# Attention on one core: steps by kind of product, minima and exponentials ahead of the transposes

## The chip, the cores and the metric

One NeuronCore of a Trainium2 chip. Its engines work from queues of their own: TensorE (PE in the profile; PEld are its weight loads), VectorE (DVE), ScalarE (ACT), GpSimd (POOL) and SyncE (SP, which issues most DMAs). The metric is the device time of one execution in microseconds, the median of three runs.

## What is computed

Three stages in a row, in float32: attention with a decay that is summed along the sequence, a routed expert layer (each token goes to one of eight experts), and a dense layer with a squared ReLU.

```python
# attention: B, H, S, D = 4, 8, 576, 64
scores = q @ k.T / sqrt(D)
cum = cumsum(log(clip(f, 1e-4, 1)))
scores = where(causal, -1e9, scores + cum[:, None] - cum[None, :])
attn = exp(scores - max(scores)); attn /= sum(attn) + 1e-9
x = (attn @ v), heads side by side            # 2304 tokens x 512
# expert layer: 8 experts, 512 -> 1024 -> 512
e = argmax(x @ w_gate); gate = softmax(x @ w_gate)[e]
y = gate * sigmoid(x @ w_output_gate)[e] * (relu(x @ w1[e]) @ w2[e])
# dense layer: 512 -> 2048 -> 512
h = relu(y @ w_in); out = (h * h) @ w_out
```

## The kernel before

The order of all instructions is written out by hand: a generator of Python code emits them, and each engine keeps the order of emission. The change lies in the first stage, attention, with the routing of its tokens.

*Pairs, chunks and units.* Two heads form a pair; there are 16 pairs, four to a batch element (`NPAIR`, `HP`). The 576 query rows of a pair are cut into five chunks (`CH`): 64 rows and four of 128, and chunk i needs 64, 192, 320, 448 or 576 key columns. A unit is one chunk of one head, and `units` lists them in the order pair, chunk, head; the last three pairs (`KL`) put their chunks 0 to 2 first and mix two units of chunks 3 and 4 in between (`KM`).

*What a unit goes through.* `products` (L301) multiplies q by k for both heads of a chunk, head 0 from partitions 0 to 63 and head 1 from 64 to 127, each into a PSUM bank of the four in `R_S`, and adds the causal mask by small bf16 products (L314, L317). `scores` (L319) is a DVE instruction that adds the decay, writes the negated scores to `pbuf` and yields their minimum; 576 columns are two pieces of 288 (`columns`), the second of which takes the first one's minimum in. `expo` (L337) is ACT's exponential in place, with the row sum. `transp` (L346) turns the exponentials by PE into one of two banks (`R_T`), up to four blocks of 128 columns at a time, and `bal.copy` takes them to `pts` by DVE or ACT, whichever a running count of costs has less on. `pv` (L365) multiplies them by v: chunks 0 to 2 together form group 0 (320 columns at most), chunks 3 and 4 group 1 (256), into the one bank of `R_O`, with head 0 on the columns 0 to 63 of the array and head 1 on 64 to 127.

*The order.* `unit(n)` emits, for each n: the loads that fall due (L624 to L631: `loadcv` and `load` two pairs ahead, and the zero fill of the expert buffers `xs_d`), the scores of unit n, the transposes of unit n - 6 (`LAG`), the exponential of unit n, and one piece of `pv`, which starts two units behind its last transposes (`PVD`). After each unit one or two pieces (`FNR`) of the routing follow:

```python
            if LAG <= n < N + LAG:
                p, i, h = units[n - LAG]
                transp(p, i, h)
```

*Routing.* When the last pair of a batch element has its PV of a group, `finish(b, g)` (L394) starts: logits by PE (lp, 32 columns of the array), transposes of the attention output (xp) with a scaling on DVE (xr), transposes of the logits (lt), a maximum and its index by small DVE operations (lg, mx, te, me, oh), ranks by small products (rp), a position for each token, and a scatter by POOL. It is cut into pieces by `yield`. `lead` finds the expert with most tokens once three batch elements are routed, and `ranks` the order of all when the last one is.

*The tail.* Six more units empty the pipeline (L935 to L943), mixed with pieces of `fnq` (the routing) and of `bp`, which splits the first expert's weights into two parts (`prep`, L735: a cast on ACT and a subtraction on DVE). Then come the end of the routing, the first expert's early products and a loop for overflowing tokens, and the expert stage.

Of the kernel before, what the change touches and what calls it, by code (L numbers as in the profile page):

```python
# [8 lines left out]
F32 = mybir.dt.float32  # L9
# [11 lines left out]
P = 128  # L21
# [13 lines left out]
LAG, PVD, FNR = 6, 2, (1, 2)  # L35
# [17 lines left out]
KL, KM = 3, 2  # L53
# [88 lines left out]
def body(ctx, tc, cst, cst16, qkv, f_in, wl_in, w12, w34, out, dbg=None):  # L142
# [39 lines left out]
    R_S, R_T, R_O, R_F, R_H, R_X = (0, 1, 2, 3), (4, 5), (6,), (7,), (0, 1), (6, 7)  # L182
# [7 lines left out]
    ptp1 = alate.enter_context(tc.tile_pool(name="ptp1", bufs=2))  # L190
    vp = alate.enter_context(tc.tile_pool(name="vp", bufs=4))
    ptp0 = aearly.enter_context(tc.tile_pool(name="ptp0", bufs=2))
# [3 lines left out]
    if True:  # L196
# [39 lines left out]
        for k in range(2):  # L236
            for h in range(2):
                for i in range(NCH):
                    if k and i < 3:
                        pbuf[k, h, i] = pbuf[0, h, i]  # L240
                        continue
                    pb = pbuf[k, h, i] = (ap2 if i < 3 else ap1).tile([P, CH[i][2] + 64], F32, name=f"p{k}{h}{i}")
                    nc.gpsimd.memset(pb[:, CH[i][2]:], 0.0)
# [13 lines left out]
        def begin0():  # L257

            cumr = ap2.tile([B * H + 1, S], F32, name="cumr")
            def spread(h, a, z):  # L260

                pp = bank(R_S, "sp")
# [22 lines left out]
        units = [(p, i, h) for p in range(NPAIR - KL) for i in range(NCH) for h in range(2)]  # L285

        u1 = [(p, i, h) for p in range(NPAIR - KL, NPAIR) for i in (3, 4) for h in range(2)]
        for p in range(NPAIR - KL, NPAIR):
            units += [(p, i, h) for i in range(3) for h in range(2)]
            if p + 1 < NPAIR:  # L290
                units += [u1.pop(0) for _ in range(KM)]
        units += u1
        begin = {units.index((p, 0, 0)): p for p in range(NPAIR)}
        mns = {}
        pps = {}

        def columns(i):
            L = CH[i][2]
            return [(0, 288), (288, 576)] if L > 512 else [(0, L)]

        def products(p, i):  # L301
# [4 lines left out]
            for a, z in columns(i):  # L306
                pp = [bank(R_S, "sp") for _ in hs]
                pps[p, i, a] = pp
                for h, s in enumerate(hs):
                    nc.tensor.matmul(pp[h][:r, 0:z - a], lhsT=t[s, 0, q0:q0 + r], rhs=t[s, 1, a:z], start=True, stop=z < L)  # L310
# [8 lines left out]
        def scores(p, i, h):  # L319
# [4 lines left out]
            pb = pbuf[p % 2, h, i]  # L324
            mn = 3.0e38
            if h == 0:
                products(p, i)
            for a, z in columns(i):
# [8 lines left out]
        def expo(p, i, h):  # L337
            b, hp = divmod(p, HP)
            q0, r, L = CH[i]
            pb = pbuf[p % 2, h, i]  # L340
# [5 lines left out]
        def transp(p, i, h):  # L346
# [9 lines left out]
            for j0, j1 in ([(0, nb)] if nb <= 4 else [(0, 3), (3, 5)]):  # L356
                tp = bank(R_T if cur[0] < N else R_T + R_S, "tp", Q4)
# [868 lines left out]
```

## Time and profile before

| | us |
|---|---|
| runs | 908.23, 909.35, 910.71; median 909.35 |
| profiled execution | 907.29 |
| its span, first to last instruction | 905.2 |
| PE busy | 874.8 (97%) |
| DVE busy | 500.0 (55%) |
| ACT busy | 405.4 (45%) |
| POOL busy | 49.5 (5%) |

A row of the timeline is a merged run of instructions of one kind: its start, how long it lasts, the engine and line, the output and its inputs, the array's rows and columns, the shape of one and how many. The end of a run of matmuls includes the time until the last result is written, so the start of the next run, not the end, says when PE went on. A float32 product appears as two matmuls, so two heads of one chunk make four. A few matmul records are missing from the trace. In a row of waits stand the engine and what it waited for, the sum, how often and the longest.

### The profile page before, as it was taken

How to read it: one execution, taken by the hardware profiler on the slowest of the kernel's cores; microseconds unless marked ns; L12 is line 12 of the kernel's file. 1: busy time of each engine (PE TensorE's matmuls, PEld its weight loads, DVE VectorE, ACT ScalarE, POOL GpSimd, SP SyncE). 2: the span in 40 equal slices, each digit the busy share in tenths (PEclk: the TensorE clock that was granted, in tenths of full speed). 3: DMA queues.
4: the chain of work that ended last, by engine and by line, in shares of the span. 5: the costliest groups of instructions: out<-in, count | busy, mean ns of one | idle time of the engine just before them, and what ended most of it. 6: DMA issues, size and time to landing. Idle time of an engine off the chain costs nothing.

```text
span 905.2 us, 15024 instructions
## 1 busy us (share of the span) xinstructions
PE 874.8 (97%) x5642; PEld 751.8 (83%) x5642; DVE 500.0 (55%) x1271; ACT 405.4 (45%) x974; POOL 49.5 (5%) x125
## 2 busy tenths in 40 slices
PE   9999999999878999999999999999999999999997
PEld 5666666666678999999999799988989999999996
DVE  5677677776637778665667888423223233233222
ACT  7656656665315555545554455223223223223221
POOL 1001111020200000000000000001100100001001
PEclk9999999999889999999999999999999999999999
DMA  8874434313346767766555443002001001000000
GB/s 256 260 251 164 147 110 159 109 58 137 112 150 219 257 206 251 244 201 213 185 193 155 123 133 94 1 3 102 36 1 36 35 1 40 31 1 12 24 1 35
DMA packets 43060, 107.40 MB, mean 119 GB/s; under 512 B 8631, under 2 KB 16695, under 8 KB 42984
## 3 DMA queue, kind: packets, MB, share of 16 engines
q1 hardware_dynamic: 39784, 96.50, 32.9%
q0 software_dynamic: 2912, 9.60, 2.9%
q8 instruction: 46, 0.75, 0.4%
q10 hardware_dynamic: 288, 0.30, 0.1%
q14 instruction: 30, 0.25, 0.1%
HBM read 84.56 MB, written 21.82 MB: 118 GB/s over the span
## 4 chain that ended last, share of the span: by engine, by line
PE 44%; issue 21%; DVE 2%; DMA 2%; POOL 1%; ACT 1%; SPq 0%; POOLq 0%; DVEq 0%; ACTq 0%
PE ph L747 22%; PE py L791 12%; PE po L1118 10%; POOL out L1129 1%; DMA raw<-w 1%; PE xp L769 1%; DMA cm_d<-xw 1%; DVE rl L1110 0%; DVE lw L879 0%; ACT hs L1111 0%; DVE xT L1052 0%; DVE hs L1112 0%; SPq L833 0%; ACT rl L1108 0%; DVE mk L880 0%
## 5 line engine op out<-in xcount | busy, mean ns | idle before, releaser
L747 PE MATMUL ph<-xT,g 128*128 128x384 f32 (+9 forms) x1968 | 346.8, 325 | 5.5 <-DMA cm_d<-xw 5.1
L747 PEld LDWEIGHTS ph<-xT,g 128*128 128x128 f32 x1968 | 322.4, 190 | 14.8 <-issue 5.3
L1118 PE MATMUL po<-g,hs 128*128 128x512 f32 x864 | 216.0, 394 | 0.8 <-ACT hs L1111 0.7
L1118 PEld LDWEIGHTS po<-g,hs 128*128 128x128 f32 x864 | 160.6, 188 | 32.0 <-ACT hs L1111 1.4
L1110 DVE TENSOR_TENSOR rl<-ph,rl 128x384 f32<-128x384 f32 x96 | 53.3, 555 | 182.8 <-ACT rl L1108 182.8
L1108 ACT ACTIVATE rl<-ph 128x384 f32<-128x384 f32 x96 | 47.2, 492 | 196.0 <-PE ph L747 193.9
L791 PE MATMUL py<-hs,g 128*128 128x288 f32 (+8 forms) x816 | 126.6, 304 | 3.9 <-DVE hs L778 2.5
L791 PEld LDWEIGHTS py<-hs,g 128*128 128x128 f32 x816 | 118.2, 190 | 4.7 <-DVE hs L778 3.1
L342 ACT ACTIVATE p<-p,mn 64x64 f32<-64x64 f32 (+4 forms) x160 | 89.3, 559 | 24.4 <-DVE mn L331 24.1
L738 DVE TENSOR_TENSOR g<-raw,g 128x512 fp32r<-128x512 f32 x126 | 81.6, 687 | 15.1 <-ACT g L737 14.0
L1112 DVE TENSOR_TENSOR hs<-rl,hs 128x384 fp32r<-128x384 f32 x96 | 53.6, 558 | 55.7 <-ACT hs L1111 55.7
L1111 ACT CAST hs<-rl 128x384 fp32r<-128x384 f32 x96 | 49.3, 513 | 72.4 <-DVE rl L1110 72.3
L331 DVE CUSTOM_DVE_ANT_0 p<-sp,cb 64x64 f32<-64x64 f32 (+4 forms) x160 | 66.2, 422 | 24.8 <-PE sp L317 19.8
L359 PE MATMUL tp<-c,p 128*128 128x128 f32 (+1 forms) x480 | 74.5, 280 | 0.5 <-DVE g L129 0.4
L737 ACT CAST g<-raw 128x512 fp32r<-128x512 f32 x126 | 71.9, 619 | 6.2 <-DMA raw<-w 6.0
L310 PE MATMUL sp<-qk 64*128 64x288 f32 (+4 forms) x384 | 70.6, 426 | 2.8 <-DVE mn L331 2.8
L777 ACT ACTIVATE hs<-ph 128x288 fp32r<-128x288 f32 (+8 forms) x68 | 28.6, 421 | 94.7 <-PE ph L747 93.2
L129 ACT COPY g<-tp 128x256 f32<-128x256 f32 (+3 forms) x111 | 45.0, 408 | 54.3 <-PE tp L359 54.2
L376 PE MATMUL po<-g,v 128*64 128x256 f32 (+3 forms) x512 | 62.2, 366 | 1.2 <-DVE g L129 1.2
L778 DVE SCALAR_TENSOR_TENSOR hs<-ph,hs 128x288 fp32r<-128x288 f32 (+8 forms) x68 | 31.8, 467 | 57.0 <-ACT hs L777 56.9
L359 PEld LDWEIGHTS tp<-c,p 128*128 128x128 f32 (+1 forms) x480 | 50.9, 140 | 10.8 <-issue 3.1
L310 PEld LDWEIGHTS sp<-qk 64*128 64x128 f32 (+1 forms) x384 | 32.9, 176 | 27.1 <-issue 19.1
(136 smaller groups left out, 597.8 us busy)
## 6 DMA issues: line engine op xcount, KB each, us to landing
raw<-w SPq DMA_DIRECT2D x63, 512.0 KB
rawc<-w SPq DMA_DIRECT2D x32, 512.0 KB
qk<-qkv SPq DMA_DIRECT2D x15, 576.0 KB
cb<-cum_d SPq DMA_DIRECT2D x15, 576.0 KB
xs_d<-zt SPq DMA_DIRECT2D x8, 826.6 KB
v<-qkv SPq DMA_DIRECT2D x16, 320.0 KB
xT<-yT_d SPq DMA_DIRECT2D x6, 768.0 KB
xw<-xs_d SPq DMA_DIRECT2D x7, 529.0 KB
```

The source lines that it names most:

```text
L310: nc.tensor.matmul(pp[h][:r, 0:z - a], lhsT=t[s, 0, q0:q0 + r], rhs=t[s, 1, a:z], start=True, stop=z < L)
L331: nc.vector.tensor_tensor_reduce(out=pb[:r, a:z], in0=pp[:r, 0:z - a], in1=cb[:r, h, a:z], scale=-SCALE, scalar=mn, op0=ALU.add, op1=ALU.m ...
L342: nc.scalar.activation(out=pb[:r, 0:L], in_=pb[:r, 0:L], func=AF.Exp, bias=mns.pop((p, i, h)), scale=-1.0, accum_out=rss[b][:r, i, hh:hh + 1])
L359: nc.tensor.transpose(tp[:, j - j0, :r], pbuf[p % 2, h, i][:r, P * j:P * j + P], ident[:r, :r])
L376: nc.tensor.matmul(po[64 * h:64 * h + 64, a:W], lhsT=v[:, j, 64 * h:64 * h + 64], rhs=pts[p, h, g][:, j, a:W], start=(j == 0), stop=(j == ...
L737: nc.scalar.copy(g[:, 0, o:o + 512], raw)
L738: nc.vector.tensor_tensor(out=g[:, 1, o:o + 512], in0=raw, in1=g[:, 0, o:o + 512].bitcast(F32), op=ALU.subtract)
L747: nc.tensor.matmul(ph[:, :n], lhsT=g[:, a, kk * 256 + f * P:kk * 256 + f * P + P], rhs=x[:, c, kk, c0:c0 + n], start=(k == 0), stop=(k == 11))
L791: nc.tensor.matmul(py[c][:, c0:c0 + cap], lhsT=g[:, a, o:o + P], rhs=hs[:, x, :cap], start=(first and n == 0), stop=(last and n == 2 and e ...
L1110: nc.vector.tensor_tensor(out=rl, in0=ph[:, :CK], in1=rl, op=ALU.mult)
L1112: nc.vector.tensor_tensor(out=hs[:, 1, :CK], in0=rl, in1=hs[:, 0, :CK].bitcast(F32), op=ALU.subtract)
L1118: nc.tensor.matmul(po[t], lhsT=hs[:, x, t * P:(t + 1) * P], rhs=g[:, a, 1024 + f * 512:1536 + f * 512], start=(first and n == 0), stop=(la ...
```

## The change

A step now is a group of chunks of a pair, both heads: group 0 has six units, group 1 four (`GR`). Of the last three pairs the three group-0 steps come first, then the three of group 1. `step(n)` emits all score products of step n, the exponentials of the last two units of step n - 1 (`rest`), then minima and exponentials of step n except the last two exponentials, then the whole of PV of step n - 2, and last the transposes of step n - 1. Score products have fixed places: banks 0 and 1 hold chunks 0 and 1, or chunk 3 and the first 64 columns of chunk 4; banks 2 and 3 hold chunk 2, or the other 512 columns of chunk 4 (`COLS`). The transposes go through banks 4, 2, 5, 3, 4, 5 in turn. Chunk 0 is transposed with all 128 rows, of which the lower ones are zeros. Pieces of the routing that contain a product (`yield 1` ahead of them) stand behind the first or the last transposed unit of a step; others also ahead of PV, behind it and behind any transposed unit that takes no product. `pbuf` exists twice for all chunks, `pts` once.

```diff
-LAG, PVD, FNR = 6, 2, (1, 2)
+GR = ((0, 1, 2), (3, 4))
+FNR = (1, 2)
...
-    R_S, R_T, R_O, R_F, R_H, R_X = (0, 1, 2, 3), (4, 5), (6,), (7,), (0, 1), (6, 7)
+    R_S, R_T, R_O, R_F, R_H, R_X = (0, 1, 2, 3), (4, 2, 5, 3, 4, 5), (6,), (7,), (0, 1), (6, 7)
...
+        steps = [(p, g) for p in range(NPAIR - KL) for g in range(2)]
+        steps += [(p, g) for g in range(2) for p in range(NPAIR - KL, NPAIR)]
+        N = len(steps)
...
+        COLS = ([(0, 64, 0, 0)], [(0, 192, 0, 64)], [(0, 320, 1, 0)], [(0, 448, 0, 0)], [(0, 64, 0, 448), (64, 576, 1, 0)])
...
-                tp = bank(R_T if cur[0] < N else R_T + R_S, "tp", Q4)
+                tp = bank((R_T[turn_t[0] % len(R_T)],), "tp", Q4)
+                turn_t[0] += 1
                 for j in range(j0, j1):
-                    nc.tensor.transpose(tp[:, j - j0, :r], pbuf[p % 2, h, i][:r, P * j:P * j + P], ident[:r, :r])
+                    nc.tensor.transpose(tp[:, j - j0, :], pbuf[side[p, i], h, i][:, P * j:P * j + P], ident)
...
+        def follow(product):
+            while fnq and (product or not due.get(id(fnq[0]), 1)):
+                try:
+                    due[id(fnq[0])] = next(fnq[0])
+                    return
+                except StopIteration:
+                    fnq.pop(0)
...
+        def step(n, then=None):
+            cur[0] = n
+            new = units(n) if n < N else []
+            old = units(n - 1) if 1 <= n <= N else []
+            if new:
+                p, g = steps[n]
...
+                for i in GR[g]:
+                    side[p, i] = n % 2
+                    advance(first)
+                    products(p, i)
+                for k in range(6 * g, 6 * g + len(new)):
+                    loads(p, k)
+            while rest:
+                expo(*rest.pop(0))
+            for k, u in enumerate(new):
+                scores(*u)
+                if k < len(new) - 2:
+                    expo(*u)
+                else:
+                    rest.append(u)
+            follow(False)
+            if n >= 2:
+                pv(*steps[n - 2])
+            follow(False)
+            turn_t[0] = 0
+            for k, u in enumerate(old):
+                transp(*u)
+                if then:
+                    then()
+                else:
+                    follow(k in (0, len(old) - 1))
...
+    def between():
+        advance(fnq, TF)
+        for _ in range(2):
+            if tail[0] in PN:
+                next(bp)
+            tail[0] += 1
+
+    step(N, between)
+    step(N + 1, between)
```

On PE, in a pair without routing, before: the transposes of chunk 4 (tp, five blocks for each head) with the second part of a PV of group 0 (po) between them, and the scores (sp) of the next chunk.

```order
L359 MATMUL tp<-c_64,p_125 128x128 x5
L376 MATMUL po<-g_2119,v 64x192
L376 MATMUL po<-g_2128,v 64x192
L376 MATMUL po<-g_2119,v 64x128
L376 MATMUL po<-g_2128,v 64x128
L359 MATMUL tp<-c_64,p_135 128x128 x5
L310 MATMUL sp<-qk 128x448 x2
```

The same place after, from a whole PV of group 0 to the next step's scores.

```order
L379 MATMUL po<-g_2098,v 64x320
L379 MATMUL po<-g_2111,v 64x320
L379 MATMUL po<-g_2098,v 64x192
L379 MATMUL po<-g_2111,v 64x192
L379 MATMUL po<-g_2098,v 64x128
L379 MATMUL po<-g_2111,v 64x128
L361 MATMUL tp<-c_64,p_143 128x128 x4
L361 MATMUL tp<-c_64,p_153 128x128 x4
L361 MATMUL tp<-c_64,p_145 128x128 x5
L361 MATMUL tp<-c_64,p_155 128x128 x5
L313 MATMUL sp<-qk 128x448 x2
```

PV is no longer cut, and the four transposed units of group 1 stand together behind it.

On ACT, before, exponentials (p, by their columns) and copies of transposes (g) alternate.

```order
L342 ACTIVATE p_135,rs<-p_135,mn 128x576
L342 ACTIVATE p_117,rs<-p_117,mn 64x64
L342 ACTIVATE p_127,rs<-p_127,mn 64x64
L342 ACTIVATE p_119,rs<-p_119,mn 128x192
L129 COPY g_2225<-tp 128x4x128
L342 ACTIVATE p_129,rs<-p_129,mn 128x192
L129 COPY g_2215<-tp 128x2x128
```

After, in a group-0 step: the two exponentials held back from the step before, four of its own, and then the copies that fall to ACT.

```order
L343 ACTIVATE p_145,rs<-p_145,mn 128x576
L343 ACTIVATE p_155,rs<-p_155,mn 128x576
L343 ACTIVATE p_117,rs<-p_117,mn 64x64
L343 ACTIVATE p_127,rs<-p_127,mn 64x64
L343 ACTIVATE p_119,rs<-p_119,mn 128x192
L343 ACTIVATE p_129,rs<-p_129,mn 128x192
L131 COPY g_2019<-tp 128x4x128
L131 COPY g_2005<-tp 128x2x128
```

Six exponentials now stand ahead of the first copy of the step.

## Rows read from the trace of the kernel before

**Rows 1.** The page: PE's granted clock in 40 slices of the span, in tenths.

```profile
PEclk9999999999889999999999999999999999999999
```

**Rows 2.** Waits, 25 to 200 us: sum, how often, longest.

```profile
ACT g L129 <- PE tp L359: 44.7, 69, 1.9
...
PE sp L310 <- DVE mn L331: 2.2, 8, 0.3
```

**Rows 3.** Timeline of PE: first scores of pairs 1, 4 and 12.

```profile
13.88 0.33 PE L310 MATMUL sp<-qk 64*64 64x64 f32 x2
...
51.24 0.33 PE L310 MATMUL sp<-qk 64*64 64x64 f32 x2
...
162.50 0.33 PE L310 MATMUL sp<-qk 64*64 64x64 f32 x2
```

**Rows 4.** Timeline of PE, 204 to 221 us, blocks of one kind.

```profile
204.97 1.30 PE L376 MATMUL po<-g,v 128*64 128x320 f32 x12
206.20 1.02 PE L310 MATMUL sp<-qk 64*128 64x448 f32 x4
207.06 0.22 PE L314 MATMUL sp<-k 64*128 64x128 bf16 x2
...
207.14 0.31 PE L359 MATMUL tp<-c,p 64*128 64x64 f32 x2
207.38 2.06 PE L376 MATMUL po<-g,v 128*64 128x256 f32 x20
209.37 1.24 PE L310 MATMUL sp<-qk 64*128 64x288 f32 x8
...
215.62 1.09 PE L359 MATMUL tp<-c,p 128*128 128x128 f32 x8
...
219.19 1.31 PE L359 MATMUL tp<-c,p 128*128 128x128 f32 x10
220.43 0.65 PE L376 MATMUL po<-g,v 128*64 128x256 f32 x2
```

**Rows 5.** Timeline of DVE: minima of 192, 288 and 448 columns.

```profile
9.18 0.36 DVE L331 CUSTOM_DVE_ANT_0 p<-sp,cb 128x192 f32<-128x192 f32 x1 [1.30 <-PE sp L317]
...
9.46 0.35 DVE L331 CUSTOM_DVE_ANT_0 p<-sp,cb 128x192 f32<-128x192 f32 x1
...
104.72 0.52 DVE L331 CUSTOM_DVE_ANT_0 p<-sp,cb,mn 128x288 f32<-128x288 f32 x1 [0.19 <-ACT p L342]
...
207.34 0.63 DVE L331 CUSTOM_DVE_ANT_0 p<-sp,cb 128x448 f32<-128x448 f32 x1 [0.33 <-PE sp L317]
...
207.89 0.62 DVE L331 CUSTOM_DVE_ANT_0 p<-sp,cb 128x448 f32<-128x448 f32 x1
```

**Rows 6.** Timeline of ACT, 108 to 110 us: exponentials.

```profile
108.08 0.78 ACT L342 ACTIVATE p<-p,mn 128x576 f32<-128x576 f32 x1 [0.77 <-DVE mn L331]
...
108.85 0.33 ACT L342 ACTIVATE p<-p,mn 64x64 f32<-64x64 f32 x1
```

**Rows 7.** Groups by shape, 25 to 200 us: busy us, mean ns, idle before.

```profile
L129 ACT COPY g<-tp 128x512 f32<-128x512 f32 x15 | 8.8, 584 | 4.1 <-PE tp L359 4.1
...
L417 DVE TENSOR_TENSOR xr<-xp,ri 128x512 f32<-128x512 f32 x12 | 8.2, 685 | 0.8 <-PE xp L410 0.6
...
L448 DVE TENSOR_REDUCE lg<-t 128x48 f32<-128x384 f32 x3 | 2.4, 804 | 0.2
```

**Rows 8.** Windows: busy of PE, PEld, DVE, ACT, POOL; clock, DMA share, GB/s.

```profile
224.00:228.00 4.00, 3.65 (x31) 3.04 (x30) 3.25 (x6) 2.68 (x6) 0.00 (x0) 1.00 0.13 37
...
232.00:234.00 2.00, 2.00 (x10) 1.15 (x10) 0.77 (x2) 0.00 (x0) 0.00 (x0) 0.50 0.69 231
```

**Rows 9.** Timeline of PE, 224 to 238 us.

```profile
224.22 0.63 PE L410 MATMUL xp<-c,ot 128*64 128x128 f32 x4
...
227.67 0.66 PE L410 MATMUL xp<-c,ot 128*128 128x128 f32 x4 [0.35 <-DVE t L443]
...
232.71 3.90 PE L376 MATMUL po<-g,v 128*64 128x256 f32 x20
```

More of the change, by code (lines that the diff above doesn't have):

```diff
@@ L284, in body, with units @@
         rss, pts, ots = {}, {}, {}
[L285 to L293, printed above, removed]
+        steps = [(p, g) for p in range(NPAIR - KL) for g in range(2)]
+        steps += [(p, g) for g in range(2) for p in range(NPAIR - KL, NPAIR)]
+        N = len(steps)
+        def units(n):
+            p, g = steps[n]
+            return [(p, i, h) for i in GR[g] for h in range(2)]
         mns = {}
[L295 to L299, printed above, removed]
+        pps, banks = {}, {}
+        COLS = ([(0, 64, 0, 0)], [(0, 192, 0, 64)], [(0, 320, 1, 0)], [(0, 448, 0, 0)], [(0, 64, 0, 448), (64, 576, 1, 0)])
         def products(p, i):
@@ L305, in products @@
             hs = [slice(64 * h, 64 * h + 64) for h in range(2)]
-            for a, z in columns(i):
-                pp = [bank(R_S, "sp") for _ in hs]
-                pps[p, i, a] = pp
+            for a, z, k, o in COLS[i]:
+                if o == 0:
+                    banks[k] = [bank((2 * k + h,), "sp") for h in range(2)]
+                pp = pps[p, i, a] = [x[:, o:o + z - a] for x in banks[k]]
                 for h, s in enumerate(hs):
-                    nc.tensor.matmul(pp[h][:r, 0:z - a], lhsT=t[s, 0, q0:q0 + r], rhs=t[s, 1, a:z], start=True, stop=z < L)
+                    nc.tensor.matmul(pp[h][:r], lhsT=t[s, 0, q0:q0 + r], rhs=t[s, 1, a:z], start=True, stop=z < L)
                 if z == L:
@@ L323, in scores @@
             q0, r, L = CH[i]
-            pb = pbuf[p % 2, h, i]
+            pb = pbuf[side[p, i], h, i]
             mn = 3.0e38
-            if h == 0:
-                products(p, i)
-            for a, z in columns(i):
+            for a, z, _, _ in COLS[i]:
                 pp = pps[p, i, a][h]
@@ L523, in body @@
         wl = ap1.tile([P, HP, 32], F32, name="wl")
[L524 to L526 removed]
+        fnq = []
+        side = {}
         V = nc.vector
@@ L642, in body @@
         for n in range(N):
-            pvq += later.pop(n, [])
-            unit(n)
-            advance(fnq, FNL if n > N - 10 else FNR[n % len(FNR)])
+            step(n)
     def weights(cm):
@@ L934, in body @@
     xT = xtp.tile([P, 2, 4, CMAX], F32R, name="xT", tag="xT")
-    for n in range(N, N + LAG):
-        pvq += later.pop(n, [])
-        unit(n)
-        pvq += later.pop(n, [])
-        if n < N + LAG - 1:
-            advance(pvq, 9)
-            advance(fnq, TF)
-        if n - N in PN:
-            next(bp)
+    tail = [0]
+    def between():
[6 more added lines that the diff above has]
+    step(N + 1, between)
     advance(fnq, PF)
-    advance(pvq, 9)
     for _ in xprep(xw, xT, CAP[0], 0, XT):
```

79 lines of the change are left out of this document (28 added, 51 removed).

## The prediction

> **What bounds the kernel now.** First the page's busy time and clock: TensorE (PE) is busy 97% of the span, and its granted clock is full but for two slices from 226 us on, where attention ends [rows 1]. But ends of matmuls are modelled, so busy is not yet work. Hence the waits next: between 25 and 200 us ScalarE (ACT) waits 44.7 us for PE's transposes, while the wait of PE's scores for VectorE (DVE) to give back a bank sums to 2.2 us [rows 2]. So PE's order sets the pace of attention. Third, the starts of chunk 0 of pairs 1, 4 and 12: three pairs without routing take 37.36 us, 12.45 each; the next eight, with the routing of two batches, 111.26, 55.6 for four [rows 3]. A batch is thus four times 12.4 plus about 6 us of routing.
>
> Fourth, what a pair's time is made of [rows 4]. A block is an uninterrupted stretch of one kind: scores (sp) use 64 rows of the array, PV (po) 64 columns, transposes (tp) all. PV of the first group (640 columns) takes 1.23 us from its start to the next kind's, PV of the second (1,088) 1.99: 1.70 ns a column, and 0.14 to 0.17 us left over in each. Eight and ten transposes last 1.09 and 1.31: 0.11 each; the ten take 1.24 to the next block, again 0.14 too much. Scores of 448 columns: 0.86 before the masks, where 448 x 1.70 is 0.76. So each change of kind costs about 0.16 us. Before, one pair is some 16 such blocks; after, 6, and 7 with the step from 64x64 to 64x128 inside the first group's scores.
>
> **The change, part by part.** *PE of a pair without routing, after*, from these rows. Scores of group 0: 576 columns 0.98, masks 0.22 (0.08 for a chunk of 128 rows), entry 0.2, and the step from chunk 0's shape to chunk 1's: 1.5 in all. That step stands nowhere in the trace, because transposes lie between; it costs between 0 and 0.17 (another change of kind), and I take 0.1, since half of the shape stays. The Trainium skill, "TensorEngine Tiling (Array Packing)", section "Tiling Modes", says that a change of tiling mode, not merely of tile, drains the engine; by that the step would cost the whole 0.17, about 1 us over 16 pairs. PV 1.23. The 18 transposes of the group before: 1.24 + 8 x 0.11 = 2.12. Group 1: 1,024 columns 1.74, masks 0.16, entry 0.2: 2.1; PV 1.99; 12 transposes 1.46. Sum 10.4 us. Chunk 0's transposes with 128 rows for 64 add nothing: the columns that stream are counted above.
>
> *Does DVE keep up?* A step's minima must end before the transposes' second and fourth tile, which take the score banks 2 and 3. 192 columns pace at 0.28, 448 at 0.55 [rows 5], so 1.05 ns a column: 64 cost 0.15, 320 0.41. The 512 of chunk 4 carry a minimum in: 0.76 by the 288-column row, after a gap of 0.19. Group 1: the first minimum starts 1.34 us into the step (448 and 64 columns, 0.2 of latency), lasts 2 x (0.55 + 0.15 + 0.19 + 0.76) = 3.3 and ends at 4.63; PE wants bank 3 at 4.7 (2.1 + 1.99 + 0.16 and four transposes). Group 0: start 1.05, 2 x (0.15 + 0.28 + 0.41) = 1.7, end 2.7; bank 2 is wanted at 3.3. *Does ACT?* 0.77 for 576 columns and 0.33 for 64 [rows 6], so 0.44 for 192 on that line. In a group-0 step it first does the two held-back 576s and then four small ones, from 0.5 (when the last copies are done) to 3.7 us; the first transposes are ready at 3.5, the second at 3.9, and DVE takes the first. So both fit, with 0.1 to 0.8 us to spare. Six tiles in four banks: the sixth waits for the third's copy (a copy of 512 takes 0.58 on ACT [rows 7]), 0.2 us. **10.6 a pair against 12.45: 1.85 saved.**
>
> *Routing* keeps its instructions, but products now stand only behind the first and the last transposed unit, so its DVE chain falls into the time in which DVE copies transposes. PE alone needs about 5.4 us a batch (20 xp and 5 lt transposes at 0.11, lp, ranks, some six changes of kind). On DVE a batch is some 8 us: five xr at 0.69, a lg of three chunks at 0.80 [rows 7] and one of two, t, and small ones. In the group-1 step with an xr, the five small operations to oh and the ranks, DVE is through the minima at 4.6 and, after lg 0.6, xr 0.7, small ones and a copy, reaches oh at 7.0; PE has finished its transposes and the 0.44 of xp at 6.1 and waits about 1 us. Bounds per batch: 5.4 (all hidden) and 11 (DVE's time over its slack added); I take 7.8, in the middle, because one such wait falls in each of the two routings and the rest has slack. Batch after: 42.4 + 7.8 = 50.2 against 55.6: 5.4.
>
> *Ends.* Pair 0 has nothing to overlap with: chunk 3 waits for the banks of chunk 1 (DVE's second minimum starts at 9.46 [rows 5]), the minima of group 1 end near 14.4, and the transposes of group 0, behind them in banks 2 and 3, near 15.3; pair 1 began at 13.88 [rows 3]. Loss 1.4. Between -0.5 and +2.
>
> Last four pairs: from 162.50 to the end of scores at 215.62 [rows 3, 4] 53.1 us. After: pair 12 10.6, its routing 7.8, then five steps and a score block: 4.95 + 4.95 + 4.2 + 4.8 + 5.55 + 2.1 = 26.55: 45. Behind it one PV of group 1 remains where one of group 0 did, 0.76 more. Gain 7.4.
>
> Tail: before, 17.1 us from 215.62 to the last PV [rows 4, 9]. After: PV 1.99, transposes 2.12, logits 0.8, PV 1.99, then four units whose copies queue on DVE with six weight subtractions (as wide as xr, so 0.69 each [rows 7]), xr and lg: 8 us more, together 15.6. Gain 1.5, between -3 and +4, since the clock's falls in the tail may shift too. Loads on SP's queue keep their order; they are issued two pairs ahead, 19 us at the new pace, and cost nothing; if that cover went, the zero fill in front of them would show in pairs 2 to 6. From the end of attention to the expert stage the work is the same chain, so it moves up as a whole.
>
> **Sum.** -1.4 + 3 x 1.85 + 2 x 5.4 + 7.4 + 1.5 = 23.9 us off the profiled execution's 907.29: 883.4. That execution lies 2.06 under the median of the runs, so 909.35 - 23.9 = **885.4 us**.
>
> **Rivals.** *Late routing* (0.18): its DVE chain lies wholly on the path, 11 a batch, and the last banks come late by 0.3 a step. For it: slack under 0.8 us. Three batches x 3.2 and 30 steps x 0.3 take back 18 at most: 891 to 903. *More than that* (0.10): routing hides at 5.4 and the tail gives 4: 32 to 34 off, 875 to 878. *DVE becomes the bound, slower* (0.08): if ACT reaches its copies only when DVE has made all six of a step, a group-0 step lasts 6.0 instead of 4.9 and a group-1 step 6.5 instead of 5.6, a pair 12.6, and routing's 8 us stand on top: 58.5 a batch, 3 more than now; with pair 0 919 us. It decides if ACT's exponentials end more than 1.5 us behind the first transposes; I found 0.2. *No change* (0.04): the 0.16 is latency that any order pays. Against it, the leftover is the same in blocks of 640 and 1,088 columns. *The clock* (0.04): transposes now come 12 or 18 at a stretch. Four us of transposes alone (224.22 to 228.33) ran at the full clock; it had fallen to the half, 1.2 GHz, by 232, after PE had also stood still, and 20 PV matmuls took 3.90 there against 2.06 at the full [rows 4, 8, 9]. A fall lasting as long as those 3.90 loses half of it, 1.9; once a pair that is 15 x 1.9 = 28, and the total 914. The Trainium skill, "TensorE: Matmul & The Clock Gate", "Part 4: PE-mode transpose", says that transposes do not count as PE activity as other matmuls do; by that rule this case is the one to fear. The 4 us at full clock speak against it, and the new stretches are 2.1 us with products on both sides. *The change not doing what it says* has no chance of its own: the order shows the blocks.
>
> **How the numbers follow.** Forecast 0.56, with 878 to 891 as its own range. 0.3%, about what a measurement of this kernel can tell from no change, is 2.7 us. Faster: 0.56 + 0.18 + 0.10 + 0.02 = 0.86; same 0.04; slower 0.08 + 0.02 = 0.10. The range reaches to the deeper gain and to the end of late routing: 874 to 903; outside lie the slower cases and some of no change.
>
> **What would show it.** Right: PE in blocks of 1.2 to 2.1 us, starts of pairs 10.4 to 10.8 apart without routing and about 50 a batch, PE's own waits only behind ranks and xp, scores ended near 193 us, clock full until then. Wrong: PE waiting before the second or fourth transposed tile in most steps (DVE bound), copies on ACT starting over 1 us behind their transposes, a granted clock under 1 before 200 us, or attention shorter by 20 while the expert stage starts no earlier.

## The result, and the profile after

The changed kernel takes **886.89 us** (median of 4 runs, 885.22 to 889.96), the kernel before beside it 908.79 (906.67 to 910.71, 4 runs): a ratio of 0.9763, 95% interval 0.9728 to 0.9799. Measured a second time in another session, five runs gave 882.35 (881.25 to 883.10) against 906.80 of before, 0.9725 (0.9705 to 0.9745). The forecast was 885.4, range 874 to 903. The execution profiled first has a span of 884.7 us where before had 905.2: 20.5 off. By the medians it is 21.9 and 24.5 us off, for 23.9 forecast. The sum is near the forecast; the terms are not, as the stages show. Starts of chunk 0 and the end of the scores are read from PE's timeline; the last column is the profile of the second session (span 881.0).

| Stretch | before | forecast gain | gain, first profile | gain, second profile |
|---|---|---|---|---|
| to the start of pair 1 | 13.88 | -1.4 | -3.51 | -2.35 |
| pairs 1 to 3 | 37.36 | 5.55 | 3.74 | 2.56 |
| pairs 4 to 11, two batches' routing | 111.26 | 10.8 | 6.72 | 10.07 |
| pair 12 to the end of the scores | 53.12 | 7.4 | 5.80 | 6.97 |
| end of the scores to the end | 689.58 | 1.5 | 7.75 | 6.95 |
| sum | 905.2 | 23.9 | 20.50 | 24.20 |

The page's clock row and the waits from 25 to 200 us, after (engine, what it waited for; sum, times, longest, us), to be read against [rows 1] and [rows 2]:

```profile
PEclk9999999999999999999999999999999999999999
```

```profile
ACT g L131 <- PE tp L361: 32.4, 46, 1.6
...
ACT p L343 <- DVE mn L332: 16.7, 18, 1.8
...
PE tp L361 <- DVE mn L332: 1.8, 4, 0.6
...
PE tp L361 <- ACT g L131: 1.5, 5, 0.4
PE tp L361 <- DVE g L131: 1.2, 3, 0.5
```

No slice of the clock is under nine tenths any more, PE still sets the pace (its transposes wait 1.8 us for minima and 2.7 for copies in 175 us), and ACT waits less for transposes than in [rows 2]. One pair without routing, pair 3, in PE's timeline (start, length, line, output and inputs, array, shape, count), where [rows 4] had some 16 blocks:

```profile
39.77 0.33 PE L313 MATMUL sp<-qk 64*64 64x64 f32 x4
...
40.06 0.59 PE L313 MATMUL sp<-qk 64*128 64x192 f32 x4
...
40.58 0.79 PE L313 MATMUL sp<-qk 64*128 64x320 f32 x4
...
41.38 1.30 PE L379 MATMUL po<-g,v 128*64 128x320 f32 x12
42.61 2.48 PE L361 MATMUL tp<-c,p 128*128 128x128 f32 x18
45.02 1.02 PE L313 MATMUL sp<-qk 64*128 64x448 f32 x4
...
45.96 1.33 PE L313 MATMUL sp<-qk 64*128 64x64 f32 x8
...
47.31 2.06 PE L379 MATMUL po<-g,v 128*64 128x256 f32 x20
49.30 1.78 PE L361 MATMUL tp<-c,p 128*128 128x128 f32 x12
51.01 0.27 PE L313 MATMUL sp<-qk 64*64 64x64 f32 x2
```

From start to start: scores 1.61, PV 1.23, 18 transposes 2.41, scores 2.29, PV 1.99, 12 transposes 1.71, together 11.24 us, where [rows 3] give 12.45 (12.36 in pairs 2 and 3) and the forecast was 10.6. PV is as forecast to the hundredth; scores are 0.30 longer, the transposes 0.54, of which 0.2 was forecast as waiting for a bank.

Scores in pair 2 before, chunk 0 and chunks 3 and 4, each with the block that follows:

```profile
38.88 0.33 PE L310 MATMUL sp<-qk 64*64 64x64 f32 x2
39.48 0.27 PE L310 MATMUL sp<-qk 64*64 64x64 f32 x1 [0.28 <-DVE mn L331]
...
39.77 0.87 PE L359 MATMUL tp<-c,p 128*128 128x128 f32 x6
...
45.81 1.02 PE L310 MATMUL sp<-qk 64*128 64x448 f32 x4
...
46.75 0.31 PE L359 MATMUL tp<-c,p 64*128 64x64 f32 x2
...
47.57 1.35 PE L310 MATMUL sp<-qk 64*128 64x288 f32 x8
...
48.94 0.44 PE L359 MATMUL tp<-c,p 128*128 128x128 f32 x2
```

Added up by kind from start to start, pair 2 before has scores 4.64, PV 3.53 and transposes 4.19 (12.36 us), pair 3 after 3.90, 3.22 and 4.12 (11.24). PV gains 0.31 for the two cuts that are gone, 0.16 each. Transposes gain only 0.07, although they stand in two blocks and not in seven. Of the scores' 0.74, 0.60 is chunk 0 (0.89 us before, 0.29 after): before, PE began its second head late, after waiting 0.28 us for a bank. Chunk 4 directly behind chunk 3 gains next to nothing: together they take 2.29 us, where 0.94 and 1.37 were 2.31 with other work between. Why is open.

Behind the scores, by stretches (columns: length, busy time of PE, PEld, DVE, ACT and POOL with the number of instructions, granted clock, DMA share, GB/s). The borders are the last score, the expert stage's first product, the second gather's transposes (xp of 96 rows), the first product behind the loop for overflowing tokens, and the second product of 400 columns. The stretches from the expert stage's first product on are called the hand-over below. First before, then after:

```profile
215.62:241.51 25.89, 20.23 (x147) 13.64 (x145) 14.51 (x41) 9.82 (x22) 0.81 (x3) 0.87 0.31 99
241.51:254.55 13.04, 12.07 (x106) 11.55 (x106) 10.98 (x45) 3.45 (x8) 5.84 (x10) 1.00 0.39 125
254.55:260.51 5.96, 0.85 (x8) 0.66 (x8) 1.02 (x2) 0.86 (x2) 0.00 (x0) 0.80 0.07 13
260.51:281.31 20.80, 17.67 (x117) 17.17 (x117) 9.97 (x19) 9.10 (x19) 0.00 (x0) 0.83 0.75 249
```

```profile
202.87:226.94 24.07, 19.08 (x156) 13.28 (x153) 16.53 (x50) 10.90 (x25) 2.10 (x6) 0.93 0.56 189
226.94:240.76 13.82, 11.82 (x106) 11.47 (x106) 9.92 (x43) 2.41 (x6) 5.84 (x10) 1.00 0.36 119
240.76:243.82 3.06, 0.85 (x8) 0.67 (x8) 1.02 (x2) 0.86 (x2) 0.00 (x0) 1.00 0.03 8
243.82:259.21 15.39, 15.39 (x116) 15.39 (x117) 7.04 (x13) 5.45 (x12) 0.00 (x0) 0.89 0.66 226
```

The reader sees that the end of attention itself gains 1.82 us (25.89 to 24.07), about the 1.5 of the forecast. The rest of the tail's gain comes where the prediction said that nothing would change: 2.90 at the loop (5.96 to 3.06) and 5.41 behind it (20.80 to 15.39), with 0.78 lost between and 1.60 given back by the end.

### The profile page after: what moved, and what is told of

It reads as the page before. It is cut to its first block, busy times and chain, and to the rows that moved or that the text cites. A ratio compares the mean times of both kernels' runs of the same rounds, so it can differ in the third digit from the quotient of the medians.

```text
span 884.7 us, 15050 instructions
## 1 busy us (share of the span) xinstructions
PE 857.2 (97%) x5642; PEld 745.6 (84%) x5642; DVE 498.7 (56%) x1266; ACT 402.8 (46%) x979; POOL 49.9 (6%) x131
## 4 chain that ended last, share of the span: by engine, by line
PE 44%; issue 22%; DVE 2%; DMA 2%; POOL 1%; ACT 1%; SPq 0%; POOLq 0%; ACTq 0%
PE ph L773 21%; PE py L817 11%; PE po L1145 10%; DMA raw<-w 1%; POOL out L1156 1%; PE xp L795 1%; DMA cm_d<-xw 1%; DVE rl L1137 0%; DVE xT L1079 0%; ACT hs L1138 0%; DVE lw L905 0%; DVE g L910 0%; ACT g L763 0%; DVE hs L1139 0%; ACT rl L1135 0%
## 5 line engine op out<-in xcount | busy, mean ns | idle before, releaser
L343 ACT ACTIVATE p<-p,mn 128x192 f32<-128x192 f32 (+4 forms) x160 | 88.4, 556 | 18.4 <-DVE mn L332 18.2
L361 PE MATMUL tp<-c,p 128*128 128x128 f32 x480 | 70.5, 281 | 8.9 <-DVE g L131 3.5
L361 PEld LDWEIGHTS tp<-c,p 128*128 128x128 f32 x480 | 51.6, 140 | 25.3 <-issue 7.4
L332 DVE CUSTOM_DVE_ANT_0 p<-sp,cb 128x192 f32<-128x192 f32 (+4 forms) x160 | 53.5, 377 | 30.5 <-PE sp L313 15.0
L313 PE MATMUL sp<-qk 64*128 64x192 f32 (+5 forms) x384 | 63.6, 438 | 0.0
L379 PE MATMUL po<-g,v 128*64 128x256 f32 (+3 forms) x512 | 55.8, 359 | 1.0 <-DVE mx L451 1.0
L131 ACT COPY g<-tp 128x256 f32<-128x256 f32 (+3 forms) x102 | 39.0, 404 | 37.7 <-PE tp L361 36.7
L1156 POOL DMA_INDIRECT out<-o,ids x18 | 17.5, 973 | 625.5 <-DVE hs L1139 360.1
```

What stands on the lines that cost most here:

```text
L313: nc.tensor.matmul(pp[h][:r], lhsT=t[s, 0, q0:q0 + r], rhs=t[s, 1, a:z], start=True, stop=z < L)
L332: nc.vector.tensor_tensor_reduce(out=pb[:r, a:z], in0=pp[:r, 0:z - a], in1=cb[:r, h, a:z], scale=-SCALE, scalar=mn, op0=ALU.add, op1=ALU.m ...
L343: nc.scalar.activation(out=pb[:r, 0:L], in_=pb[:r, 0:L], func=AF.Exp, bias=mns.pop((p, i, h)), scale=-1.0, accum_out=rss[b][:r, i, hh:hh + 1])
L361: nc.tensor.transpose(tp[:, j - j0, :], pbuf[side[p, i], h, i][:, P * j:P * j + P], ident)
L379: nc.tensor.matmul(po[64 * h:64 * h + 64, a:W], lhsT=v[:, j, 64 * h:64 * h + 64], rhs=pts[p, h, g][:, j, a:W], start=(j == 0), stop=(j == ...
```

## The experiments

Twelve runs followed. Where a run's stages are compared with the changed kernel, its second profile is taken (pairs without routing 11.2 us, a batch element of four pairs 50.76 and 50.43), because the first one lost 1.6 us in pair 6 and 1.75 in pair 10 to something that the order does not explain (last section).

### Two more changes of kind a step

```diff
...
-            if n >= 2:
-                pv(*steps[n - 2])
+            pq = [pv(*steps[n - 2])] if n >= 2 else []
+            advance(pq, 1 if n < 2 * (NPAIR - KL) else 2)
...
                 transp(*u)
+                if k == 0:
+                    advance(pq, 2)
...
```

> The changed kernel, with the PV of steps 2 to 25 cut in two: its first block of keys stands ahead of the first transposed unit, the rest behind it. No instruction is added; each of 24 steps gets two more changes of kind on PE. Theory (the gain comes from fewer changes of kind, at about 0.16 us each): 48 x 0.16 = 7.7 us longer, the span 884.7 to about 892.4, and a pair without routing 11.2 to 11.85 us. Rival (the gain comes from the four banks and from minima and exponentials standing ahead of the transposes, and PE has slack that hides a change of kind): longer by less than 1.5 us, a pair by less than 0.15.

Measured 889.90 us, 0.9819 of before (0.9788 to 0.9850). Pair 3 now has the first block of PV and the first transposes apart:

```profile
46.78 0.76 PE L379 MATMUL po<-g,v 128*64 128x320 f32 x4
47.47 0.66 PE L361 MATMUL tp<-c,p 128*128 128x128 f32 x4
48.05 0.76 PE L379 MATMUL po<-g,v 128*64 128x192 f32 x8
48.75 2.04 PE L361 MATMUL tp<-c,p 128*128 128x128 f32 x14
```

The pair takes 11.79 us for 11.24, 0.14 for each of its four more changes. From the start of pair 2 to the end of the scores it is 177.35 us (33.44 to 210.79) against 169.76 (28.61 to 198.37): 7.59 more for 44 more changes of kind, **0.17 us each**. The theory's number holds, also where routing is under way (a batch element takes 52.99 and 53.24 us for 50.76 and 50.43, with 16 more changes), and the rival falls: PE has no slack that hides a change of kind. By the medians the run is 7.55 us over the changed kernel's second measurement and 3.01 over its first.

### Two banks for the transposes in place of four

```diff
-    R_S, R_T, R_O, R_F, R_H, R_X = (0, 1, 2, 3), (4, 2, 5, 3, 4, 5), (6,), (7,), (0, 1), (6, 7)
+    R_S, R_T, R_O, R_F, R_H, R_X = (0, 1, 2, 3), (4, 5, 4, 5, 4, 5), (6,), (7,), (0, 1), (6, 7)
```

> The changed kernel, with its transposes in two banks (4, 5, 4, 5, 4, 5) in place of four; all else as it is. Theory A (the order of kinds alone gives the gain): within 1.5 us of the changed kernel, pairs 11.2 us. Theory B (long blocks of transposes need the banks): a tile of the group-1 chunks takes PE 0.44 us, its copy 0.58 on ACT or 0.69 on DVE, so two banks turn over in about 1.2 us for two tiles, 0.6 a tile; six tiles last about 3.1 us where they now take 2.41, and the smaller group 0 about 0.4 longer: 0.6 to 1.1 us a pair, 9 to 16 us in all, the wait of PE's transposes for copies named in the trace.

Measured 903.42 us, 0.9964 (0.9945 to 0.9982). Some 21 us of the gain are gone by the second measurement of the changed kernel, 16.5 by the first. PE's transposes in pair 3, with their waits in brackets:

```profile
45.74 0.94 PE L361 MATMUL tp<-c,p 128*128 128x128 f32 x5 [0.44 <-DVE g L131]
...
53.55 0.87 PE L361 MATMUL tp<-c,p 128*128 128x128 f32 x6 [0.30 <-DVE g L131]
```

The 18 transposes last 3.37 us (44.21 to 47.58) for 2.41, the 12 last 2.50 (51.86 to 54.36) for 1.71, and a pair takes 12.99: more than the 12.45 of before [rows 3]. Theory B holds, above its own bound of 1.1 a pair. Up to the end of the scores this run is even 2.30 us longer than the kernel before (217.92 for 215.62); what it gains comes behind them (682.08 us to the end for 689.58), where the changed kernel gains as well. So in attention fewer changes of kind bring nothing if the long blocks they make stand still for copies.

### Minima, transposes and exponentials in turn

With two banks as in the run before this one.

```diff
-            while rest:
-                expo(*rest.pop(0))
-            for k, u in enumerate(new):
-                scores(*u)
-                if k < len(new) - 2:
-                    expo(*u)
-                else:
-                    rest.append(u)
...
             if n >= 2:
                 pv(*steps[n - 2])
...
-            for k, u in enumerate(old):
-                transp(*u)
+            for k in range(max(len(new), len(old))):
+                if k < len(new):
+                    scores(*new[k])
+                if k < len(old):
+                    transp(*old[k])
+                if k < len(new):
+                    expo(*new[k])
...
```

> The changed kernel with two banks for the transposes as in the run beside it, and with minimum, transposed unit and exponential emitted in turn, unit by unit, as the kernel before did; PE's order is unchanged. Theory A (the order of kinds alone): no more than 1.5 us over the run with two banks. Theory C (minima ahead of the copies matter): a copy then stands behind a minimum of 0.35 to 0.75 us on DVE or an exponential of 0.4 to 0.8 on ACT, each of six tiles waits about 0.2 to 0.4 more, and the last minima free the score banks late: 1 to 2 us a pair over the run with two banks, 15 to 30 us in all, so that most of the gain of the change is lost.

Measured 969.26 us, 1.0717 (1.0666 to 1.0768): 66 us over the run with two banks, more than twice what theory C gave. The waits of this kernel from 25 to 250 us, and DVE's rows behind a PV:

```profile
ACT ot L131 <- PE po L379: 48.4, 11, 6.1
...
DVE ot L131 <- PE po L379: 45.9, 14, 4.6
```

```profile
62.05 0.42 DVE L131 COPY ot<-po 128x256 f32<-128x256 f32 x1 [3.30 <-PE po L379]
62.39 0.61 DVE L332 CUSTOM_DVE_ANT_0 p<-sp,cb 128x448 f32<-128x448 f32 x1
```

Its reason is partly another than I had named. With the minima emitted behind PV, the copy of PV's result (ot) stands ahead of them in DVE's or ACT's queue. The engine stands 3.30 us until PV is done, while score products that ended long before wait behind that copy. These waits make 94 us in 225, not all on the path; the granted clock falls as well, 0.89 over that stretch. So the run shows that, on two banks, minima and exponentials have to stand ahead of PV's copy and the transposes' copies; it parts neither the two copies nor minima from exponentials, and the same order on four banks was not run.

### Routing behind every transposed unit

```diff
-                    follow(k in (0, len(old) - 1))
+                    follow(True)
```

> The changed kernel, with pieces of the routing that contain a product allowed behind every transposed unit, as all pieces were before, in place of the first and the last unit of a step. Theory (two places matter because PE otherwise waits in the middle of its transposes for the routing's small DVE operations): 0.5 to 1.5 us a batch element more, 1.5 to 4 us in all, with waits of PE for t, oh or xr inside the transposes. Rival (the places don't matter, since a piece costs PE the same anywhere): within 1.5 us; or it is better by 1 to 2 us, since routing ends earlier.

Measured 889.89 us, 0.9811 (0.9775 to 0.9847). A batch element takes 52.61 and 52.93 us for 50.76 and 50.43, the last four pairs to the end of the scores 50.86 for 46.15: 9.1 us, where at most 4 were expected. In PE's timeline of pair 4 a transposed row of attention now comes while the bank it needs is still being read:

```profile
68.56 0.66 PE L410 MATMUL xp<-c,ot 128*128 128x128 f32 x4 [1.05 <-DVE xr L417]
```

By the stages two places a step are worth more than the theory gave them. This profile is of the slowest of the four runs; by the medians the run is 7.5 us over the second measurement of the changed kernel and 3.0 over the first, and the latter lies in the expected range. That also bears on the prediction's rival of late routing: what was feared there happens with more places.

### The first step chunk by chunk

```diff
                     products(p, i)
+                    if n == 0:
+                        for h in range(2):
+                            scores(p, i, h)
+                            if i < 2:
+                                expo(p, i, h)
...
```

> The changed kernel, with minima and exponentials of the very first step emitted chunk by chunk between its score products, as the kernel before had them, and not behind all products; the last two exponentials still move to the next step. Theory (pair 0 lost 3.4 us because DVE's first minimum starts at 9.59 us, behind ACT's copy of the last decay columns, and PE then waits for score banks): the first minimum starts near 7.7, PE gets to chunk 3 before 10, pair 1 begins at 15.3 to 15.9 in place of 17.39, and the end comes 1.5 to 2 us earlier. Rival (the clock falls to the half there whatever the order): pair 1 stays at 17 or later.

Measured 882.13 us, 0.9713 (0.9686 to 0.9739), not told apart from the changed kernel's 0.9725. Pair 1 starts at 17.47: the rival. The first minimum starts at 8.24 us (forecast 7.7) and chunk 3 at 10.45 (forecast before 10). The granted clock from 9 to 13 us says why, in the run of this section and in the tail's run below, whose start is the changed kernel's:

```profile
9.00:13.00 4.00, 4.00 (x32) 2.81 (x31) 1.59 (x9) 3.19 (x12) 0.00 (x0) 0.68 0.67 234
```

```profile
9.00:13.00 4.00, 3.26 (x29) 2.11 (x23) 3.37 (x19) 3.87 (x15) 0.00 (x0) 1.00 0.92 313
```

Where the clock stays full (second line), pair 1 starts at 15.57 us, near the prediction's 15.3. Where it falls to the half, 1.2 GHz, it starts at 17.47 here and at 17.39 in the first profile of the changed kernel (0.53 from 10 to 13 us). So some 1.8 of that profile's 3.51 us belong to the clock. Whether the order of this section gains anything at the full clock is not shown: the clock fell in both profiles that have it (this one and that of the edits together). The fall comes in some executions of either kernel: also in the profiles of all three variants of the kernel before that were run, though not in the one that the prediction was made from.

### A fifth bank where no routing is under way

```diff
+    R_T7 = (4, 2, 5, 3, 7, 4)
...
-                tp = bank((R_T[turn_t[0] % len(R_T)],), "tp", Q4)
+                tp = bank(((R_T if fnq else R_T7)[turn_t[0] % len(R_T)],), "tp", Q4)
```

> The changed kernel, with bank 7 as the fifth bank of the transposes wherever no routing is under way (4, 2, 5, 3, 7, 4 for 4, 2, 5, 3, 4, 5). Theory (pairs take 11.2 and not the forecast 10.6 us partly because the fifth and sixth tile wait for copies): 18 transposes go from 2.41 to about 2.15 us and 12 from 1.68 to about 1.5, a pair without routing to 10.75 us, and with some seven such pairs the end comes 2.5 to 4 us earlier. Rival (the wait is for exponentials or lies at the changes of kind): pairs stay within 0.1 of 11.2.

Measured 882.54 us, 0.9726 (0.9704 to 0.9748): the same as the changed kernel. In pair 3, from the start of the 18 transposes to the next scores:

```profile
40.41 2.19 PE L362 MATMUL tp<-c,p 128*128 128x128 f32 x18
42.53 1.02 PE L314 MATMUL sp<-qk 64*128 64x448 f32 x4
```

2.12 us, exactly the forecast's sum without a bank wait, and pairs take 10.87. But only pairs 1 to 3 have it; pairs 7 and 11 stay at 11.16, since some piece of routing was still in the queue there. So the theory holds for a pair and is worth 1 us by the pairs' starts, not 2.5.

### The weights' splits later in the tail

```diff
-XA, NA, RA, PK, PN, AP = 208, 4, (2, 2, 3, 3, 2, 9), (20, 21), (0, 1, 2, 3, 4, 5), (4, 6, 10, 12, 15, 15)
+XA, NA, RA, PK, PN, AP = 208, 4, (2, 2, 3, 3, 2, 9), (20, 21), (6, 7), (4, 6, 10, 12, 15, 15)
...
-    advance(fnq, PF)
+    for _ in range(PF):
+        advance(fnq)
+        next(bp)
```

> The changed kernel, with the six splits of the first expert's weights in the tail moved: two behind the last transposed unit, four between the next pieces of the routing, in place of two behind each of the first three units. Theory (in the tail PE waits 2.31 us for a copy that stands on ACT and DVE behind these splits, 1.03 us more for the last PV, and the clock falls after it): both waits go, the last PV starts 3 us earlier, and the end comes 2 to 4 us earlier. Rival (the splits are needed by then, or the gathered tokens set the start of the expert stage): the end within 1 us.

Measured 883.19 us, 0.9741 (0.9705 to 0.9777). The last transposes and the last PV, in the first profile of the changed kernel (two rows) and in this run (two rows):

```profile
215.72 0.44 PE L361 MATMUL tp<-c,p 128*128 128x128 f32 x2 [2.31 <-DVE g L131]
...
218.20 3.43 PE L379 MATMUL po<-g,v 128*64 128x256 f32 x18 [1.03 <-DVE mx L451]
```

```profile
207.32 0.44 PE L361 MATMUL tp<-c,p 128*128 128x128 f32 x2 [0.24 <-DVE g L131]
208.12 2.49 PE L379 MATMUL po<-g,v 128*64 128x256 f32 x20
```

The wait goes as the theory says, and the expert stage starts 21.9 us behind the scores (196.55 to 218.45) for 24.07. To the end it keeps 1.8 to 2.6 us, by this profile against the two of the changed kernel; its runs scatter from 878.42 (this profile's) to 886.00 and don't show that.

### Products of zeros in the tail of the kernel before

```diff
+    warm(R_S, 14)
     advance(fnq, PF)
...
             for _ in xprep(xw, xT, CAP[0], XT):
                 pass
+            warm(R_H, 22)
```

> The kernel before, with 14 and 22 more products of zeros at two places of its tail where PE stood still ahead of a fall of the clock (behind the last transposed unit, and behind the second gather's transposes), so that PE is at work there. Theory (the tail of the changed kernel gained 7.8 us and not 1.5 because before the clock was at the half for 17.1 us at the end of attention and in the hand-over, and after for 6.8 there): the clock stays up at 231 to 237 and at 258 to 264 us, and the kernel before gets 3 to 5 us faster, near 904. Rival (weights or the gather set the pace of the hand-over): within 1.5 us of before.

Measured 908.95 us, 1.0019 (1.0004 to 1.0035): the theory falls. The first fall of the clock was avoided and PE's tail came 1.3 us earlier by the ranks' products (239.22 for 239.44 us, with attention 1.1 later), but the second only moved. PE at the loop:

```profile
255.92 4.91 PE L180 MATMUL wu<-z 128*128 128x512 bf16 x22
266.42 3.94 PE L747 MATMUL ph<-xT,g 128*128 128x192 f32 x17 [5.58 <-DMA cm_d<-xw]
```

PE stands 5.58 us after its own last product, as it stood 5.11 in the kernel before (254.55 to 260.51 above), although it now arrives 5 us later. So this stop begins when PE gets to the loop, and work put ahead of it delays what follows.

### The kernel before without two early splits

```diff
-XA, NA, RA, PK, PN, AP = 208, 4, (2, 2, 3, 3, 2, 9), (20, 21), (0, 1, 2, 3, 4, 5), (4, 6, 10, 12, 15, 15)
+XA, NA, RA, PK, PN, AP = 208, 4, (2, 2, 3, 3, 2, 9), (), (0, 1, 2, 3, 4, 5), (4, 6, 10, 12, 15, 15)
```

> The kernel before, without the two splits of weights that it makes during the last pieces of the routing, ahead of the loop for overflowing tokens; they come behind it, as in the changed kernel, where that place in the order is never reached. Theory (the hand-over gained 4.95 us between its first and second 400-column product because before had used up one more tile of weights by then, and ACT, and behind it PE, stood until the next one landed): the wait of 5.6 us on ACT for raw weights near 270 us goes, the second 400-column product follows the first after about 4 us and not 8.9, and the kernel gets 2 to 4 us faster. Rival (the weights come at the pace of the DMA queues whatever is split when): the wait moves on and the time stays within 1 us.

Measured 905.91 us, 0.9978 (0.9963 to 0.9994). ACT before, and the two products of 400 columns, before and in this run:

```profile
274.20 1.14 ACT L737 CAST g<-raw 128x512 fp32r<-128x512 f32 x2 [5.63 <-DMA raw<-w]
```

```profile
272.42 2.43 PE L747 MATMUL ph<-xT,g 128*128 128x400 f32 x12
...
281.31 2.74 PE L747 MATMUL ph<-xT,g 128*128 128x400 f32 x12
```

```profile
275.43 2.43 PE L747 MATMUL ph<-xT,g 128*128 128x400 f32 x12
...
279.37 2.44 PE L747 MATMUL ph<-xT,g 128*128 128x400 f32 x12
```

The wait is gone, and the second product follows after 3.94 us for 8.89, as in the changed kernel. In the two other variants of the kernel before, which keep the splits in place, ACT still waits for raw weights there (6.18 us in the next section's run, 2.53 in the one with products of zeros). So 4.95 us of the hand-over's gain come from the tail's shorter queue of routing pieces: in the changed kernel the places 20 and 21, at which before made two splits ahead of the loop, are never reached. In time it is 0.9 us at the median, which is what the rival forecast. In the profile the stop at the loop was longer (5.77 us) and the clock behind it at the half (0.50 from 261 to 267 us, 0.67 before); whether that took the rest is not shown.

### The kernel before with a third bank

```diff
-                tp = bank(R_T if cur[0] < N else R_T + R_S, "tp", Q4)
+                tp = bank((R_T if fnq else (4, 5, 7)) if cur[0] < N else R_T + R_S, "tp", Q4)
```

> The kernel before, with bank 7 as a third bank of the transposes wherever no routing is under way; PE's order is unchanged. Theory (in short blocks the copies keep up, and PE is held by changes of kind, not by banks): pairs without routing stay at 12.4 us, the time within 1 us. Rival (two banks hold before back as well, and the four banks alone give much of the change's gain): such pairs get 0.3 us or more shorter, 2 us or more in all.

Measured 907.13 us, 1.0000 (0.9986 to 1.0015), pairs without routing 12.36 as before. In short blocks two banks are enough, and a third gives nothing; four were not tried in that order. Beside the run on two banks: the new order without the banks is worth 0.4%, none of it in attention, a bank without the new order nothing, and the whole change 2.4 to 2.8%.

### The changed kernel again, and the edits together

> The changed kernel once more, beside the three others on one chip, so that they have a base: 885 to 888 us. Theory (the profiled execution of the changed kernel lost 1.6 us in pair 6 and 1.6 in pair 10, and 2 in pair 0, to things that other executions of the same order don't have): these three pairs come out at 13.0, 13.0 and 9.1 us in some executions and longer in others, and the median lies 1 to 3 us under 886.9. Rival: they repeat, and the median stays within 1 us of 886.9.

Measured 882.35 us (above). Pairs 6 and 10 take 13.00 and 13.01 us, not 14.60 and 14.76; pair 0 takes 9.46, and the clock falls as pair 1 begins (0.60 from 15 to 17 us, 0.55 from 17 to 19), which pair 1 pays for (12.38). The theory holds, and the median lies 4.5 us under 886.9, more than the 1 to 3 expected. Pairs 6 and 10 make 3.35 of them; what the rest is stays open. Both values stand for the change.

```diff
...
+                if n == 1:
+                    warm(R_F, 4)
...
```

> The changed kernel with the three edits together (first step chunk by chunk, bank 7 for transposes where no routing is under way, splits of weights later in the tail) and four products of zeros on PE ahead of the second step's scores, where PE waits for a score bank and the clock fell in some executions. Expected from the single runs: bank 7 about 1 us (0.31 in three pairs), the tail 2 to 3, the first step 0.4, the clock in pair 0 up to 2: 4 to 6 us under the changed kernel beside it, near 881. If the single runs' gain over 886.9 was only scatter between sessions, it stays within 2 us of it.

Measured 881.10 us, 0.9712 (0.9691 to 0.9733), against 882.35 on the same chip: 1.25 us less, where 4 to 6 were expected, and the intervals don't separate it. In its profile pairs 1 to 3 take 10.94, 10.87 and 10.86 us and the way from the scores to the end 680.4 for 682.6, but the clock fell in pair 0 in spite of the four products, and pair 1 began at 18.46. So the gains of bank 7 and of the tail are there in their stages, those of the first step and of the four products are not, and the sum does not beat the scatter of the whole.

## Why the prediction was right, point by point

*What bounds the kernel, and the price of a change of kind.* Right between PV and transposes: 0.16 forecast, 0.17 measured by adding 44 changes, 0.16 by taking out the two cuts of PV. The rival of no change, that any order pays this latency, falls with it. It did not come out where score chunks now stand directly behind one another (chunks 3 and 4: 2.29 us for 2.31).

*A pair without routing.* 10.6 forecast, 11.2 measured. The mis-sized terms are the scores (1.61 and 2.29 for 1.5 and 2.1) and the transposes. With a fifth bank the 18 take 2.12, as in the sum, so their excess of 0.29 is the bank wait, to which the forecast gave 0.2 a pair; the 12 take 1.63 even then, for 1.46. Of the scores' 0.30, 0.19 is in the second group (2.29 for 2.1), where putting chunk 4 behind chunk 3 was to save an entry and did not; what it and the step between array shapes in the first group cost, the runs do not part.

*DVE and ACT keep up.* Right, with little to spare, as said: PE waited 1.8 us in all for minima in the first profile, 0.3 in the second. The runs with two banks and with the mixed order show what lies on the other side: 16.5 to 21 us, and 66 more. The prediction treated banks and order as conditions to be met by 0.1 to 0.8 us; it did not price them, and they are what the gain stands on.

*Routing.* 7.8 a batch forecast. The two batches less eight pairs at 11.2 leave 7.5 in the first profile and 5.8 in the second, near the lower bound of 5.4. In the second the forecast was too high, and the rival of late routing falls.

*Ends.* Pair 0: 15.3 forecast for the start of pair 1, 15.57 where the clock holds, 17.39 in the first profile. The order was priced right; that the clock can fall there was a point the prediction gave no price. Last four pairs: 7.4 forecast, 5.80 and 6.97 measured. The tail to the expert stage: 1.5 forecast, 1.82 measured. The forecast's own terms (1.99, 2.12, 0.8, 1.99 and 8) add up to 14.9 and not to 15.6, so they gave 2.2, and the whole sum 24.6.

*"It moves up as a whole".* This step was wrong: 5.9 us more came behind it. Shown are the 4.95 us between two products that ACT's wait for weights cost, and which go when two splits come later; how much of them reaches the end is not shown, since the same edit alone gave 0.9. Of the 2.90 at the loop one run shows that the stop counts from PE's arrival; why it lasts 5.1 to 5.8 us in the kernel before and its three variants and about 2.2 in the changed one and most of its variants (5.4 in the mixed order) stays open.

*The clock on transposes.* The granted clock is 1.00 from 25 to 200 us, with 12 to 18 transposes at a stretch:

```profile
25.00:200.00 175.00, 168.12 (x1575) 115.80 (x1576) 132.95 (x528) 115.15 (x378) 17.54 (x48) 1.00 0.49 159
```

The rule of the Trainium skill ("TensorE: Matmul & The Clock Gate", "Part 4: PE-mode transpose"), that transposes don't count as busy time as products do, would have made this the case to fear; in blocks of up to 2.4 us between products this trace does not show it.

*The signs it named.* Of those for being right, pairs 10.4 to 10.8 us apart (11.2) and scores ended near 193 us (202.87 and 198.37) did not come, and about 50 a batch did in the second profile (52.3 and 50.6). One of those for being wrong came, a granted clock under 1 before 200 us, but in the first step and not on transposes.

So the direction and the mechanism were right, but that the total came within 1.5 and 3.1 us of the two medians is luck, because errors of both signs met: attention gained 12.75 us in the first profile and 17.25 in the second for 22.4 forecast, and the hand-over, to which the prediction gave nothing, made up most of the difference.

## What to carry to other kernels

Grouping TensorE's work by array shape paid about 0.16 us here for each change between PV and transposes that it saved (next to nothing between two score chunks), but only where PSUM banks and the order on the copying engines let the longer blocks run through: price the turn-over of a bank (fill, copy, free) against the block before regrouping. Keep what frees input banks ahead of copies that wait for a later product, since a queue that keeps its order carries one wait into everything behind it (DVE stood 3.30 us for one such copy). And when a stage's pieces are placed by counting positions in another queue, shortening that queue moves them: here it took two weight splits past a loop and, by accident, five microseconds out of one stretch, of which 0.9 reached the end when it was done alone.

## What the runs showed of the hardware

*The clock's fall is not a property of the order.* The same start fell in some executions and held in others, 1.8 us apart at pair 1 (17.39 and 15.57), and products of zeros placed by the idle times of one profile avoided one fall of two (before) or none (pair 0).

*A stop at the loop.* After the last product ahead of a loop whose count comes from data, PE stood about 2.2 us in the changed kernel and most of its variants and 5.1 to 5.8 in the kernel before and its variants. The Trainium skill ("Runtime: NRT & Kernel Launch", "Instruction fetch mechanics") says that a branch to a page that isn't at hand has to wait for it to be fetched; no run here shows what PE waited for.

*DVE standing with its inputs ready.* In the first profile of the changed kernel, pair 6, chunk 2's first minimum starts at 81.43 us, 1.18 us after DVE's last instruction and 2.1 us after the chunk's last mask product ended (79.29); in the second, with the same order, DVE goes on to it without a gap:

```profile
81.43 0.49 DVE L332 CUSTOM_DVE_ANT_0 p<-sp,cb 128x320 f32<-128x320 f32 x1 [1.18 <-PE tp L361]
```

```profile
79.62 0.48 DVE L332 CUSTOM_DVE_ANT_0 p<-sp,cb 128x320 f32<-128x320 f32 x1
```

POOL issues its scatters in that time in both, so they alone don't explain it. Pair 6 took 1.6 us more there and pair 10 1.75, and the cause is open.
